# One ring of five 4 MB buffers for K, V and the weights of a decode step, in place of three pools of 1 and 2 MB buffers

## The chip, the cores and the metric

The kernel runs on one core of one Trainium2 chip. Times are microseconds (us) of device time, the median of several executions. "Before" is the kernel as it was, "changed" the kernel with the change. The span of a profile (first to last instruction) is up to about 2 us shorter than the reported time of the same execution.

## The reference, cut to what matters

One decode step for four sequences: attention over a cache of 8192 keys with 32 heads of 128, a gated feed-forward layer beside it, and a gate that mixes the two.

```python
# x: (4, 1, 1024)   k_cache, v_cache: (4, 32, 8192, 128) bf16, 268 MB each
q = (x @ wq).reshape(B, 1, 32, 128).transpose(0, 2, 1, 3)
p = softmax(einsum("bhqd,bhkd->bhqk", q, k_cache) * 128 ** -0.5)
a = einsum("bhqk,bhkd->bhqd", p, v_cache) ... @ wo            # wq, wo: 8.4 MB each
b = x + sigmoid(x @ w_r) * ((silu(x @ w_gate) * (x @ w_up)) @ w_down)   # 7.3 MB each
out = g * a + (1 - g) * b          # g = sigmoid(sum(x * gate_w))
```

Each K and V element is read once and used once. There are 575.7 MB to read and very little to compute on them.

## The kernel before

The parts that the change touches. Each of the 128 (sequence, head) units has one K transfer and one V transfer of 2 MB, in runs of 16 KB per partition. Weights come in 1 MB chunks, in runs of 1 KB (wq, gate, up) or 2 KB (down, wo).

```python
    GH = 8                                   # heads per softmax group
    LAG = GH + 3                             # V units behind K units
    wst = ctx.enter_context(tc.tile_pool(name="wst", bufs=3))
    knp = ctx.enter_context(tc.tile_pool(name="knp", bufs=2))
    vnp = ctx.enter_context(tc.tile_pool(name="vnp", bufs=3))
    # ... cut ...
        for b in range(Bn):                  # two-byte elements
            nc.sync.dma_start(out=xT[:, :, b], in_=x2[b].rearrange("(t c) -> c t", c=P))
        nc.sync.dma_start(out=wrg[:, :, 0], in_=B_w_r.rearrange("(t c) -> c t", c=P))
        nc.sync.dma_start(out=wrg[:, :, 1], in_=gate_w.rearrange("(t c) -> c t", c=P))
    # ... cut ...
    def w_in_chunk(view, c0, psum_view, t0):             # WCOLS = 512: 1 KB runs
        def emit():
            wc = wst.tile([P, DT, WCOLS], BF, tag="w")
            nc.sync.dma_start(out=wc[:], in_=view[:, :, c0:c0 + WCOLS])
            # ... 32 products of 128 x 128 weights with 4 columns ...
    # ... cut ...
    def k_unit(u):
        kn = knp.tile([P, J, Dh], BF, name="kn")
        nc.sync.dma_start(out=kn[:], in_=A_k_cache[b, h].rearrange("(p j) d -> p j d", p=P))
        T = ttp.tile([P, J, 2, 32, 2], BF, name="T")
        nc.vector.transpose(out=T[:]..., in_=kn[:]...)   # frees the K buffer
        # ... 16 products with T; at the 8th head of a group: softmax(g)
    def v_unit(u):
        vn = vnp.tile([P, J, Dh], BF, name="vn")
        nc.sync.dma_start(out=vn[:], in_=A_v_cache[b, h].rearrange("(p j) d -> p j d", p=P))
        # ... 16 products, a copy on ACT, 4 small products that transpose the head's output
```

The end of it: eleven V units without K units beside them, then wo in eight chunks, eight transposes, a copy and the output.

Of the kernel before, what the change touches and what calls it, by code (L numbers as in the profile page):

```python
# [9 lines left out]
BF = mybir.dt.bfloat16  # L10
F32 = mybir.dt.float32
# [8 lines left out]
def kernel(  # L20
# [14 lines left out]
):  # L35
    nc = tc.nc
# [4 lines left out]
    assert Sq == 1 and Dh == P and D % P == 0 and F % P == 0 and Sk % P == 0  # L41
    DT, FT, J = D // P, F // P, Sk // P
    GH = 8
    NJC = 4
    JJ = J // NJC
    assert J % NJC == 0 and JJ * 32 <= 512 and NJC * GH == 32 and JJ % 4 == 0
    LAG = GH + 3
    WPK = 2
    NU = Bn * H
    assert NU % GH == 0 and H % GH == 0 and H * Bn <= 128  # L50
    NG = NU // GH
    ZW = 128 * (GH - 1) + 31 + 128 + 1
# [5 lines left out]
    wst = ctx.enter_context(tc.tile_pool(name="wst", bufs=3))  # L58
    knp = ctx.enter_context(tc.tile_pool(name="knp", bufs=2))
    ttp = ctx.enter_context(tc.tile_pool(name="ttp", bufs=2))  # L60
    vnp = ctx.enter_context(tc.tile_pool(name="vnp", bufs=3))
    ptp = ctx.enter_context(tc.tile_pool(name="ptp", bufs=3))
    osp = ctx.enter_context(tc.tile_pool(name="osp", bufs=2))
    stat = ctx.enter_context(tc.tile_pool(name="stat", bufs=3))
    shrp = ctx.enter_context(tc.tile_pool(name="shrp", bufs=1, space=PSUM))
    scp = ctx.enter_context(tc.tile_pool(name="scp", bufs=2, space=PSUM))
    ops = ctx.enter_context(tc.tile_pool(name="ops", bufs=2, space=PSUM))
    o2p = ctx.enter_context(tc.tile_pool(name="o2p", bufs=2, space=PSUM))
    fps = ctx.enter_context(tc.tile_pool(name="fps", bufs=1, space=PSUM))

    ident = const.tile([P, P], BF)
    make_identity(nc, ident[:])
    identf = const.tile([P, P], F32)
    make_identity(nc, identf[:])
    R = const.tile([P, 4, P], BF)
    nc.gpsimd.memset(R[:], 0.0)
    for he in range(4):
        half, e = divmod(he, 2)
        nc.gpsimd.affine_select(out=R[:, he, :], in_=R[:, he, :], compare_op=ALU.not_equal, fill=1.0,
                                base=-(64 * half + e), pattern=[[0, 4], [-2, 32]], channel_multiplier=1)  # L80
    mask8 = const.tile([P, GH], F32)
    nc.gpsimd.memset(mask8[:], 0.0)
    for m in range(P // GH):
        nc.gpsimd.affine_select(out=mask8[:], in_=mask8[:], compare_op=ALU.not_equal, fill=1.0,
                                base=-GH * m, pattern=[[-1, GH]], channel_multiplier=1)
    pen8 = const.tile([P, GH], F32)
    nc.vector.tensor_scalar(out=pen8[:], in0=mask8[:], scalar1=-1.0, scalar2=3.0e38, op0=ALU.add, op1=ALU.mult)

    xT = const.tile([P, DT, Bn], BF)
    wrg = const.tile([P, DT, 2], BF)  # L90
    with nc.allow_non_contiguous_dma(reason="tiny transposed loads of x / w_r / gate_w"):
        for b in range(Bn):
            nc.sync.dma_start(out=xT[:, :, b], in_=x2[b].rearrange("(t c) -> c t", c=P))
        nc.sync.dma_start(out=wrg[:, :, 0], in_=B_w_r.rearrange("(t c) -> c t", c=P))
        nc.sync.dma_start(out=wrg[:, :, 1], in_=gate_w.rearrange("(t c) -> c t", c=P))
    wrep = const.tile([P, 2, DT, P], BF)
    for i in range(2):
        nc.vector.tensor_copy(out=wrep[:, i, :, :], in_=wrg[:, :, i:i + 1].to_broadcast([P, DT, P]))
# [4 lines left out]
    hT = const.tile([P, FT, Bn], BF)  # L103
    sgb = const.tile([P, 2, Bn], F32)
    c12 = const.tile([P, 2, Bn], F32)
    baseT = const.tile([P, DT, Bn], F32)
    Zt = [const.tile([P, 4, ZW], BF, name=f"Z{i}") for i in range(2)]
    for z in Zt:
        nc.gpsimd.memset(z[:], 0.0)

    shr = shrp.tile([P, 512], F32)
    nc.vector.memset(shr[:], 0.0)
    o0 = 0
    gu_ps = shr[:, o0:o0 + 2 * FT * Bn].rearrange("p (w t b) -> p w t b", w=2, t=FT); o0 += 2 * FT * Bn
    q_ps = shr[:, o0:o0 + H * Bn].rearrange("p (h b) -> p h b", h=H); o0 += H * Bn
    yT_ps = shr[:, o0:o0 + DT * Bn].rearrange("p (t b) -> p t b", t=DT); o0 += DT * Bn
    rg_ps = shr[:, o0:o0 + 2 * Bn].rearrange("p (w b) -> p w b", w=2); o0 += 2 * Bn
    aT_ps = shr[:, o0:o0 + DT * Bn].rearrange("p (t b) -> p t b", t=DT); o0 += DT * Bn
    assert o0 <= 512

    def mm_acc(out_ap, lhsT, rhs):
        nc.tensor.matmul(out_ap, lhsT=lhsT, rhs=rhs, start=False, stop=True, skip_group_check=True)  # L122

    for i in range(2):
        for t in range(DT):
            mm_acc(rg_ps[:, i, :], wrep[:, i, t, :], xT[:, t, :])
    nc.scalar.activation(out=sgb[:], in_=rg_ps, func=ACT.Sigmoid)
    nc.vector.tensor_scalar(out=c12[:, 0, :], in0=sgb[:, 1, :], scalar1=-1.0, scalar2=1.0, op0=ALU.mult, op1=ALU.add)
    nc.vector.tensor_tensor(out=c12[:, 1, :], in0=c12[:, 0, :], in1=sgb[:, 0, :], op=ALU.mult)

    WCOLS = 4 * P
    wqv = A_wq.rearrange("(t c) n -> c t n", c=P)
    wgv = B_w_gate.rearrange("(t c) f -> c t f", c=P)
    wuv = B_w_up.rearrange("(t c) f -> c t f", c=P)
    wdv = B_w_down.rearrange("(t f) n -> f t n", f=P)
    wov = A_wo.rearrange("(h d) n -> d h n", d=P)
    assert (H * Dh) % WCOLS == 0 and F % WCOLS == 0
    TCH = max(1, 4096 // D)

    def w_in_chunk(view, c0, psum_view, t0):  # L140
        def emit():
            wc = wst.tile([P, DT, WCOLS], BF, tag="w")
            nc.sync.dma_start(out=wc[:], in_=view[:, :, c0:c0 + WCOLS])
            for ci in range(WCOLS // P):
                for t in range(DT):
                    mm_acc(psum_view[:, t0 + ci, :], wc[:, t, ci * P:(ci + 1) * P], xT[:, t, :])
        return emit

    def w_out_chunk(view, r0, nrow, psum_view, rhs_of):
        def emit():  # L150
            wc = wst.tile([P, TCH, D], BF, tag="w")
            nc.sync.dma_start(out=wc[:, :nrow, :], in_=view[:, r0:r0 + nrow, :])
            for rr in range(nrow):
                for nt in range(DT):
                    mm_acc(psum_view[:, nt, :], wc[:, rr, nt * P:(nt + 1) * P], rhs_of(r0 + rr))
        return emit

    for h0 in range(0, H, WCOLS // P):
        w_in_chunk(wqv, h0 * P, q_ps, h0)()
    nc.vector.tensor_copy(out=qT[:], in_=q_ps)  # L160
    qa_ps = ops.tile([P, 4, H * Bn], F32, name="o_ps")
    for he in range(4):
        nc.tensor.matmul(qa_ps[:, he, :], lhsT=R[:, he, :], rhs=qT[:].rearrange("p h b -> p (h b)"),
                         start=True, stop=True)
    nc.vector.tensor_copy(out=qa[:].rearrange("p e h b -> p e (h b)"), in_=qa_ps[:])

    wjobs = []
    for f0 in range(0, FT, WCOLS // P):
        wjobs.append(("g", w_in_chunk(wgv, f0 * P, gu_ps[:, 0], f0)))
    for f0 in range(0, FT, WCOLS // P):  # L170
        wjobs.append(("u", w_in_chunk(wuv, f0 * P, gu_ps[:, 1], f0)))

    def h_job():
        g_sb = stat.tile([P, FT, Bn], F32, tag="g_sb")
        nc.scalar.activation(out=g_sb[:], in_=gu_ps[:, 0], func=ACT.Silu)
        nc.vector.tensor_tensor(out=hT[:], in0=g_sb[:], in1=gu_ps[:, 1], op=ALU.mult)
    wjobs.append(("h", h_job))
    for t0 in range(0, FT, TCH):
        wjobs.append(("d", w_out_chunk(wdv, t0, min(TCH, FT - t0), yT_ps, lambda t: hT[:, t, :])))

    def base_job():
        nc.vector.tensor_tensor(out=baseT[:], in0=xT[:], in1=c12[:, 0:1, :].to_broadcast([P, DT, Bn]), op=ALU.mult)
        ty = stat.tile([P, DT, Bn], F32, tag="ty")
        nc.vector.tensor_tensor(out=ty[:], in0=yT_ps, in1=c12[:, 1:2, :].to_broadcast([P, DT, Bn]), op=ALU.mult)
        nc.vector.tensor_tensor(out=baseT[:], in0=baseT[:], in1=ty[:], op=ALU.add)
    wjobs.append(("b", base_job))

    S_ps = {}
    PT_t = {}
    rinv_t = {}  # L190
    oT2_t = {}

    def build_strips(g):
        b, h0 = divmod(g * GH, H)
        Z = Zt[g % 2]
        for he in range(4):
            for a in range(4):
                c0 = 31 + 32 * a
                dst = Z[32 * a:32 * a + 32, he, c0:c0 + 128 * (GH - 1) + 1:128]
                nc.gpsimd.tensor_copy(out=dst, in_=qa[32 * a:32 * a + 32, he, h0:h0 + GH, b])  # L200

    def k_unit(u):
        b, h = divmod(u, H)
        g, h8 = divmod(u, GH)
        if h8 == 0:
            build_strips(g)
            S_ps[g] = scp.tile([P, JJ * 32], F32, name="S_ps")
        sps = S_ps[g]
        Z = Zt[g % 2]
        kn = knp.tile([P, J, Dh], BF, name="kn")  # L210
        nc.sync.dma_start(out=kn[:], in_=A_k_cache[b, h].rearrange("(p j) d -> p j d", p=P))
        T = ttp.tile([P, J, 2, 32, 2], BF, name="T")
        nc.vector.transpose(out=T[:].rearrange("p j h i e -> p (j h i e)").bitcast(U32),  # L213
                            in_=kn[:].rearrange("p j d -> p (j d)").bitcast(U32))
        n = 0
# [7 lines left out]
        if h8 == GH - 1:  # L223
            softmax(g)
# [129 lines left out]
```

## Time and profile before

| what | value | view |
|---|---|---|
| time | 1384.77 us (1384.01 to 1385.76) | times |
| DMA queue 1 | 575.71 MB, busy 99.5% of 16 engines | page, part 3 |
| PE, DVE | busy 82% and 44% of the span | page, part 1 |
| mean rate | 416 GB/s | page, part 2 |

This is the page's table of the span in 40 slices for the kernel before (busy tenths of the DMA engines, the rate in each slice, all packets by size), and the line of the queue that carries the data (packets, MB, share of 16 engines):

```profile
DMA  9999999999999999999999999999999999999997
GB/s 307 410 403 422 394 430 420 431 418 431 420 430 421 430 431 427 431 424 430 419 430 429 425 431 426 430 420 430 429 430 430 427 429 417 431 431 431 399 385 268
DMA packets 73973, 576.61 MB, mean 416 GB/s; under 512 B 10932, under 2 KB 33460, under 8 KB 41144
...
q1 hardware_dynamic: 73912, 575.71, 99.5%
```

The engines are "busy" all the time, so the busy share says nothing about what can be gained. The rate does: slices of 430 and 431 stand beside slices of 394 to 420. The view of stretches of the same kernel (stretch, length, busy time and count of PE, PE loads, DVE, ACT and POOL, granted clock, DMA share, GB/s) puts the losses into four places:

```profile
0.00:10.00 10.00, 0.75 (x16) 0.58 (x16) 2.47 (x6) 1.46 (x2) 1.20 (x9) 1.00 0.65 106
10.00:100.00 90.00, 52.99 (x765) 30.96 (x766) 27.83 (x9) 1.28 (x1) 18.28 (x56) 0.84 1.06 402
100.00:160.00 60.00, 43.57 (x372) 20.45 (x371) 30.89 (x19) 2.32 (x4) 4.18 (x18) 0.76 0.99 402
160.00:1300.00 1140.00, 983.02 (x4640) 443.17 (x4639) 549.44 (x261) 75.95 (x144) 55.00 (x237) 0.95 1.00 427
1300.00:1360.00 60.00, 52.09 (x272) 25.51 (x270) 1.41 (x6) 7.09 (x13) 0.40 (x1) 1.00 0.97 377
1360.00:1384.70 24.70, 9.74 (x273) 8.88 (x272) 1.24 (x4) 0.57 (x1) 0.00 (x0) 0.60 0.63 224
```

The loss in the middle is a small one at each of 16 softmaxes. In this piece of the timeline (start us, duration, engine, line, instruction, idle time before it and its releaser), DVE holds both K buffers while it waits for the group's maximum from POOL and the row sums from ACT; the next K transfer is issued only when the first late transpose ends:

```profile
670.91 0.69 DVE L229 TENSOR_REDUCE m_4110<-S_ps 128x1 f32<-128x512 f32 x1 [5.91 <-PE S_ps L220]
674.43 0.37 POOL L234 PARTITION_ALL_REDUCE gmx<-mex  x1
675.41 0.69 ACT L243 ACTIVATE PTs<-S_ps,negm 128x512 bf16<-128x512 f32 x1 [9.23 <-DVE negm L240]
677.10 8.72 DVE L213 STREAM_TRANSPOSE T<-kn 128x4096 uint32<-128x4096 uint32 x2
681.52 0.33 SPq L211 DMA_DIRECT2D kn<-in_A_k_cache_dram  x1
```

To compare kernels I use one more number, the **deficit**: a time on the trace less the time that the bytes moved so far would take at 431 GB/s (each packet's bytes spread over its recorded duration, the data queues alone). All 575.7 MB would take 1335.7 us, so the span of a kernel is 1335.7 us plus its final deficit. The kernel before has a deficit of 18.2 us at 160 us, 29.7 at 1300 us and 49.0 at its end.

### The profile page before, as it was taken

To read this page: it belongs to the slowest core of one execution; us is meant where nothing else is said; L and a number is where in the kernel's file an instruction comes from. 1 tells how busy PE (TensorE), PEld (TensorE's weight loads), DVE (VectorE), ACT (ScalarE), POOL (GpSimd) and SP (SyncE) were. 2 spreads that over 40 slices of the span, in tenths; PEclk is the share of its full clock that TensorE was granted. 3 is DMA by queue.
4 is the path that set the end of the run, shared out by engine and by line. 5 is a ranking of instruction groups with operands and counts; after the bars stand their busy time and mean duration, and the time that the engine had idled before them with its cause. 6 is when DMAs were issued, how large, how long until landed. Compare 5 with 4: busy or idle time off the path is not lost.

```text
span 1384.7 us, 14348 instructions
## 1 busy us (share of the span) xinstructions
PE 1142.2 (82%) x6332; PEld 529.5 (38%) x6332; DVE 613.3 (44%) x303; ACT 88.7 (6%) x165; POOL 79.1 (6%) x320
## 2 busy tenths in 40 slices
PE   2676889979797988979797997979797997989885
PEld 2333333434343433434343443434343343434443
DVE  1335545454535345444444445444454535354300
ACT  0000000000000000000000000000000000000110
POOL 3101010010101010010101000010101000000000
PEclk9877889999999999999999999999999999999997
DMA  9999999999999999999999999999999999999997
GB/s 307 410 403 422 394 430 420 431 418 431 420 430 421 430 431 427 431 424 430 419 430 429 425 431 426 430 420 430 429 430 430 427 429 417 431 431 431 399 385 268
DMA packets 73973, 576.61 MB, mean 416 GB/s; under 512 B 10932, under 2 KB 33460, under 8 KB 41144
## 3 DMA queue, kind: packets, MB, share of 16 engines
q1 hardware_dynamic: 73912, 575.71, 99.5%
q8 instruction: 49, 0.80, 0.2%
q14 instruction: 12, 0.10, 0.0%
HBM read 575.68 MB, written 0.01 MB: 416 GB/s over the span
## 4 chain that ended last, share of the span: by engine, by line
PE 61%; DMA 17%; DVE 10%; ACT 4%; POOL 4%; issue 3%; SPq 0%; ACTq 0%; DVEq 0%; POOLq 0%
PE S_ps L220 28%; PE o_ps L266 25%; DMA kn<-in_A_k_cache_dram 14%; DVE T L213 9%; ACT o_sb L270 4%; POOL Z_188 L200 2%; POOL Z_189 L200 2%; DMA wc<-in_A_wq_dram 1%; DMA wc<-in_A_wo_dram 1%; DVE PT L251 1%; PE oT_7480 L275 1%; PE shr L122 1%; PE oT_5562 L275 1%; PE oT_2338 L275 1%; PE oT_1935 L275 1%
## 5 line engine op out<-in xcount | busy, mean ns | idle before, releaser
L213 DVE STREAM_TRANSPOSE T<-kn 128x4096 uint32<-128x4096 uint32 x128 | 566.8, 4435 | 445.0 <-DMA kn<-in_A_k_cache_dram 434.8
L266 PE MATMUL o_ps<-vn,PT 128*4 128x512 bf16 x2048 | 463.2, 379 | 0.0
L220 PE MATMUL S_ps<-T,Z_188 128*128 128x512 bf16 x1024 | 264.5, 414 | 34.0 <-DVE T L213 34.0
L220 PE MATMUL S_ps<-T,Z_189 128*128 128x512 bf16 x1024 | 258.2, 407 | 35.2 <-DVE T L213 35.1
L266 PEld LDWEIGHTS <-PT 128*4 128x4 bf16 x2048 | 167.9, 87 | 280.5 <-issue 49.6
L220 PEld LDWEIGHTS <-Z_188 128*128 128x128 bf16 x1024 | 102.1, 104 | 167.5 <-issue 76.3
L220 PEld LDWEIGHTS <-Z_189 128*128 128x128 bf16 x1024 | 100.6, 102 | 164.3 <-issue 68.8
L270 ACT COPY o_sb<-o_ps 4x512 f32<-4x512 f32 x128 | 73.3, 572 | 1006.2 <-PE o_ps L266 1006.2
L200 POOL COPY Z_188<-qa 32x8 bf16<-32x8 bf16 x128 | 27.1, 211 | 529.5 <-PE S_ps L220 512.9
L200 POOL COPY Z_189<-qa 32x8 bf16<-32x8 bf16 x128 | 27.0, 211 | 499.0 <-PE S_ps L220 493.7
L122 PEld LDWEIGHTS <-wc 128*128 128x128 bf16 x1184 | 34.1, 101 | 54.5 <-DMA wc<-in_A_wq_dram 15.4
L122 PE MATMUL shr<-xT,wc 128*128 128x4 bf16 x704 | 21.8, 166 | 32.6 <-DMA wc<-in_A_wq_dram 14.7
L243 ACT ACTIVATE PTs<-S_ps,negm 128x512 bf16<-128x512 f32 x16 | 11.0, 687 | 165.1 <-DVE negm L240 165.1
L236 DVE TENSOR_TENSOR gmm<-gmx,mask_118 128x8 f32<-128x8 f32 x16 | 2.7, 167 | 41.7 <-POOL gmx L234 41.7
L282 DVE TENSOR_TENSOR OT<-oT_7480,rinv 128x8 bf16<-128x8 f32 x1 | 0.2, 176 | 42.5 <-PE oT_7480 L275 42.5
L122 PE MATMUL shr<-OT,wc 128*128 128x4 bf16 x256 | 7.8, 166 | 11.1 <-DMA wc<-in_A_wo_dram 11.1
L275 PE MATMUL oT_1532<-identf,o_sb 4*128 4x1 f32 x64 | 9.0, 258 | 7.2 <-ACT o_sb L270 7.2
L234 POOL PARTITION_ALL_REDUCE gmx<-mex x16 | 5.9, 368 | 156.4 <-DVE mex L232 148.8
L275 PE MATMUL oT_2338<-identf,o_sb 4*128 4x1 f32 x64 | 8.4, 248 | 7.3 <-ACT o_sb L270 7.3
L275 PE MATMUL oT_5562<-identf,o_sb 4*128 4x1 f32 x64 | 8.4, 248 | 7.3 <-ACT o_sb L270 7.3
L275 PE MATMUL oT_6368<-identf,o_sb 4*128 4x1 f32 x64 | 8.4, 248 | 7.3 <-ACT o_sb L270 7.3
L275 PE MATMUL oT_1935<-identf,o_sb 4*128 4x1 f32 x64 | 8.4, 248 | 7.3 <-ACT o_sb L270 7.3
(122 smaller groups left out, 302.5 us busy)
## 6 DMA issues: line engine op xcount, KB each, us to landing
kn<-in_A_k_cache_dram SPq DMA_DIRECT2D x128, 2048.0 KB, 14.8
vn<-in_A_v_cache_dram SPq DMA_DIRECT2D x128, 2048.0 KB, 16.3
wc<-in_A_wq_dram SPq DMA_DIRECT2D x8, 1024.0 KB, 7.7
wc<-in_A_wo_dram SPq DMA_DIRECT2D x8, 1024.0 KB, 8.5
wc<-in_B_w_gate_dram SPq DMA_DIRECT2D x7, 1024.0 KB, 11.9
wc<-in_B_w_up_dram SPq DMA_DIRECT2D x7, 1024.0 KB, 12.0
wc<-in_B_w_down_dram SPq DMA_DIRECT2D x7, 1024.0 KB, 11.6
xT<-in_A_x_dram SPq DMA_DIRECT2D x4, 2.0 KB, 3.2
```

Of the source, the lines that this page charges most:

```text
L122: nc.tensor.matmul(out_ap, lhsT=lhsT, rhs=rhs, start=False, stop=True, skip_group_check=True)
L200: nc.gpsimd.tensor_copy(out=dst, in_=qa[32 * a:32 * a + 32, he, h0:h0 + GH, b])
L213: nc.vector.transpose(out=T[:].rearrange("p j h i e -> p (j h i e)").bitcast(U32), in_=kn[:].rearrange("p j d -> p (j d)").bitcast(U32))
L220: nc.tensor.matmul(sps[:, :], lhsT=Z[:, he, s:s + P], rhs=T[:, JJ * jc:JJ * (jc + 1), half, :, e], start=(h8 == 0 and n == 0), stop=(h8 == ...
L234: nc.gpsimd.partition_all_reduce(gmx[:], mex[:], channels=P, reduce_op=bass_isa.ReduceOp.max)
L236: nc.vector.tensor_tensor(out=gmm[:], in0=gmx[:], in1=mask8[:], op=ALU.mult)
L243: nc.scalar.activation(out=PTs[:], in_=sps[:], func=ACT.Exp, bias=negm[:, 0:1], scale=scale, accum_out=rs[:, 0:1])
L251: nc.vector.transpose(out=PT[:].rearrange("p j c h -> p (j c h)"), in_=PTs[:])
L266: nc.tensor.matmul(o_ps[:, :], lhsT=PT[:, 4 * uq:4 * uq + 4, jc, h8], rhs=vn[:, j0:j0 + 4, :], start=(n == 0), stop=(n == J // 4 - 1))
L270: nc.scalar.copy(out=o_sb[:], in_=o_ps[:])
L275: nc.tensor.matmul(oT2[:, h8:h8 + 1], lhsT=o_sb[0:4, t * Dh:(t + 1) * Dh], rhs=identf[0:4, t:t + 1], start=(t == 0), stop=(t == 3))
L282: nc.vector.tensor_tensor(out=OT[:, h0:h0 + GH, b], in0=oT2[:, 0:GH], in1=rinv[:, :], op=ALU.mult)
```

## The change

Its intent: few, long transfers that never wait. K, V and all weights go through one pool of five 4 MB buffers. A piece of K or V is two heads, a contiguous 32 KB per partition; the weights are regrouped so that a partition reads 28 or 32 KB of contiguous rows (down 8 KB, wo still 2 KB). V follows K by four pieces. The small inputs become 16-byte runs and move to the ACT queue. The products that transpose a head's output are put off into the next piece, and wo and down multiply with the activations as the stationary side, so that the result needs no transposes at the end.

```diff
-    wst = ctx.enter_context(tc.tile_pool(name="wst", bufs=3))
-    knp = ctx.enter_context(tc.tile_pool(name="knp", bufs=2))
-    vnp = ctx.enter_context(tc.tile_pool(name="vnp", bufs=3))
+    ring = ctx.enter_context(tc.tile_pool(name="ring", bufs=5))
...
-            nc.sync.dma_start(out=xT[:, :, b], in_=x2[b].rearrange("(t c) -> c t", c=P))
-        nc.sync.dma_start(out=wrg[:, :, 0], in_=B_w_r.rearrange("(t c) -> c t", c=P))
+        nc.scalar.dma_start(out=xT[:], in_=x2.rearrange("b (c t) -> c b t", t=DT))
+        nc.scalar.dma_start(out=wrg[:, 0, :], in_=B_w_r.rearrange("(c t) -> c t", t=DT))
...
-            nc.sync.dma_start(out=wc[:], in_=view[:, :, c0:c0 + WCOLS])
+        w = slot()[:, :TW * H * Dh].rearrange("p (t h d) -> p t h d", t=TW, h=H)
+        nc.sync.dma_start(out=w.rearrange("p t h d -> p t (h d)"), in_=wqv[:, t0:t0 + TW, :])
...
+        return cache[b, h0:h0 + HT].rearrange("h (r j) d -> (h r) (j d)", j=JR)
...
-        kn = knp.tile([P, J, Dh], BF, name="kn")
-        nc.sync.dma_start(out=kn[:], in_=A_k_cache[b, h].rearrange("(p j) d -> p j d", p=P))
+        kn = slot()
+        nc.sync.dma_start(out=kn[:], in_=kv_view(A_k_cache, u))
+        for c in range(JR // CJ):            # four transposes per piece
...
-    while ik < NU: weights(WPK); k_unit(ik); ik += 1; v_unit(iv); iv += 1
+    for u in range(NT + LAG):
+        if u < NT:
+            k_piece(u)
+        if u >= LAG:
+            v_piece(u - LAG)
+        if side:
+            side.pop(0)()                    # one weight piece
+    for nh in (16, 12, 3, 1):                # wo, by heads
+        if h0 + nh <= H:
+            wo_piece(h0, nh)
...
```

(The removed loop is drawn together on one line; cuts are marked.)

## The prediction

> **What bounds the kernel now.** The DMA engines. In the queue view queue 1 is busy 99.5% of 16 engines (575.7 MB, mean 416 GB/s); PE is busy 82%, DVE 44%. The chain of waits names mostly PE (61%) because PE consumes last; in steady state the transfers end last (DVE waits 435 us for K). Where the mean loses to the best rate, 431 GB/s (225-265 and 620-665 us), by the view of stretches:
>
> - 0-10 us: 106 GB/s, 7.5 us lost. Six loads of x, w_r and gate_w in two-byte elements precede the first weights, issued only at 4.95 us.
> - 10-150 us: 383-409 GB/s, 11 us lost: weights in 1 KB runs (46 ns a packet against 611 ns for 16 KB, packet records: 38 ns per KB plus 8) and, at 140-145 us, 259 GB/s after the first softmax.
> - 150-1250 us: 427-428, about 9 us: at each of 16 softmaxes the two K buffers come free late (period 78.5 us for 33.55 MB, 77.9 at 431).
> - 1300-1360 us: 377 GB/s, 7.5 us: eleven V units left over, each 5.32 us on PE (3.6 of products, the ACT copy, transposing products), while their data needs 4.87 us.
> - 1360-1385 us: 224 GB/s, 12 us: wo waits for buffers, then transposes, output.
>
> Sum 47 us; 575.7 MB at 431 GB/s would be 1336 us.
>
> **What the change does.** Bytes stay. All streams share five 4 MB buffers, so a transfer waits for the piece five before it, which landed some 39 us (four pieces of 9.7 us) earlier. A K piece is freed after four transposes (8.9 us, 2 x 4.43 now), a V piece after 32 products (7.2 us at 226 ns): both far inside 39 us, so softmax should not reach the queue. Per pair of pieces (19.5 us) PE needs 14.4 us, DVE 8.9 plus softmax: neither becomes the limit. Weight runs grow to 8-32 KB (wo stays at 2). Small loads go to another queue. LAG falls to 4 pieces and the transposing products are put off, so a left-over V piece costs PE 7.2 us against 9.7 of DMA.
>
> **Sum.** Start 2.6 us (0.7 to issue, 1.9 to the first packet, as now). 575.7 MB at 431: 1335.7 us. The Trainium skill, "DMA: Bandwidth & Descriptors", section "Where 436 GB/s comes from", gives a ceiling of 435.2 GB/s; if what is missing at 16 KB is a fixed cost per packet, 32 KB gives 433, 1329.6 us. I take 432: 1332.6. wo's 2 KB runs: +0.6. Tail after the last landing: wo's 12-head piece lands 2.5 us before the end and needs 24 products, then 8 more: 32 x 0.226 = 7.2, so 4.7 us over; copy 0.7, output and end 2.6: 8 us. Total about 1343 us, 3% faster. All of it is on the critical path, since the DMA queue is that path.
>
> **What would show it.** Slices at 430-433 GB/s from first to last but one, no dip at softmax; K/V packets of 32 KB near 1210 ns; SyncE waiting for buffers with DMA full; weights at over 425 GB/s; only the last 8 us low.
>
> **What would make it wrong.** 32 KB runs that are slower or split (streams further apart in HBM), rate below 428; strided weight loads for gate/up, or a cold PE clock (0.5) making V pieces (32 x 0.43 = 13.7 us) and the wo tail slow; a dependence in the ring that serializes K and V; a queue that starves in the first pieces.
>
> Range 1333 to 1356 us. Chances: faster by over 2% 0.86, within 2% 0.12, slower 0.02.

## The result

The changed kernel takes 1361.18 us (1361.15 to 1361.58, four runs), the kernel before 1384.94 us in the same rounds; the ratio is 0.9835, with a 95% interval of 0.9821 to 0.9849. It is 1.6 to 1.7% faster. The prediction was 1343 us with a range of 1333 to 1356, so it was 18 us too low.

The page of the changed kernel, the same lines:

```profile
DMA  9999999999999999999999999999999999999996
GB/s 398 389 431 430 428 430 431 432 430 430 431 431 430 430 430 431 432 431 431 430 431 431 431 431 431 431 431 431 431 432 431 431 430 430 430 430 431 430 425 237
DMA packets 25278, 576.49 MB, mean 424 GB/s; under 512 B 3068, under 2 KB 3076, under 8 KB 7176
...
q1 hardware_dynamic: 24392, 575.68, 98.9%
```

The middle is flat now, as predicted: no dips at the softmaxes. The busy share fell a little while the kernel became faster. What is left is at the two ends. The stretches of the changed kernel:

```profile
0.00:10.00 10.00, 0.00 (x0) 0.00 (x0) 0.48 (x1) 1.28 (x1) 0.86 (x6) 1.00 0.91 351
10.00:40.00 30.00, 0.00 (x0) 0.00 (x0) 0.00 (x0) 0.00 (x0) 4.68 (x12) 1.00 0.99 421
40.00:60.00 20.00, 12.35 (x281) 8.46 (x282) 6.22 (x13) 1.46 (x2) 1.56 (x8) 1.00 0.91 358
60.00:160.00 100.00, 82.32 (x718) 41.89 (x717) 53.91 (x32) 3.94 (x6) 6.53 (x27) 0.88 1.01 430
160.00:1300.00 1140.00, 970.52 (x4228) 408.85 (x4226) 559.55 (x351) 60.79 (x103) 70.55 (x269) 0.94 1.00 431
1300.00:1330.00 30.00, 25.26 (x128) 12.11 (x129) 0.24 (x1) 2.30 (x4) 0.00 (x0) 1.00 0.99 416
1330.00:1359.90 29.90, 25.46 (x104) 9.79 (x103) 0.92 (x2) 1.15 (x2) 0.00 (x0) 0.89 0.60 217
```

The line of 10 to 40 us shows the first surprise: PE and DVE did nothing at all in it, though the first weights (4 MB) had landed by 14 us, by the semaphore times. The deficits, stage by stage, of the two kernels (and of the two best experiments, told below):

| stage | before | changed | x_first | tail8 |
|---|---|---|---|---|
| 0 to 160 us | 18.2 | 7.2 | 4.3 | 4.3 |
| 160 to 1300 us | 11.5 | 1.6 | 1.5 | 1.5 |
| 1300 us to the end | 19.3 | 15.4 | 14.5 | 12.1 |
| span less 1335.7 us | 49.0 | 24.2 | 20.3 | 17.9 |

So the change won 11.0 us at the start, 9.9 in the middle and 3.9 at the end.

### The profile page after: what moved, and what is told of

Same layout as the page of the kernel before. It is cut to its first block, busy times and chain, and to the rows that moved or that the text cites. A ratio compares the mean times of both kernels' runs of the same rounds, so it can differ in the third digit from the quotient of the medians. Undisturbed runs are those within 1.5% of the kernel's fastest.

```text
span 1359.9 us, 12458 instructions
## 1 busy us (share of the span) xinstructions
PE 1115.9 (82%) x5456; PEld 481.1 (35%) x5456; DVE 621.3 (46%) x399; ACT 70.9 (5%) x118; POOL 84.2 (6%) x322
## 4 chain that ended last, share of the span: by engine, by line
DMA 44%; PE 39%; DVE 11%; issue 4%; ACT 1%; POOL 0%; ACTq 0%; DVEq 0%
DMA piece<-in_A_k_cache_dram 38%; PE S_ps L252 17%; PE o_ps L304 17%; DVE T L245 11%; DMA wrg<-in_B_w_r_dram 3%; DMA piece<-in_A_wo_dram 3%; PE acc L140 2%; PE shr L140 2%; PE oT L317 1%; ACT o_sb L310 1%; DVE OT L322 0%; DVE wrep L146 0%; POOL PB_128 L282 0%; ACT PTs L275 0%; DVE PT L277 0%
## 5 line engine op out<-in xcount | busy, mean ns | idle before, releaser
L245 DVE STREAM_TRANSPOSE T<-piece 128x2048 uint32<-128x2048 uint32 x256 | 577.3, 2291 | 487.9 <-DMA piece<-in_A_k_cache_dram 390.0
L252 PE MATMUL S_ps<-T,Z_126 128*128 128x512 bf16 x1024 | 281.8, 429 | 92.9 <-DVE T L245 92.6
L252 PE MATMUL S_ps<-T,Z_127 128*128 128x512 bf16 x1024 | 264.0, 408 | 54.5 <-DVE T L245 54.5
L304 PE MATMUL o_ps<-piece,PB_129 128*8 128x512 bf16 x1024 | 227.9, 381 | 2.0 <-DMA piece<-in_A_v_cache_dram 1.9
L304 PE MATMUL o_ps<-piece,PB_128 128*8 128x512 bf16 x1024 | 226.2, 379 | 0.0
L304 PEld LDWEIGHTS <-PB_129 128*8 128x8 bf16 x1024 | 86.9, 87 | 139.0 <-issue 16.3
L304 PEld LDWEIGHTS <-PB_128 128*8 128x8 bf16 x1024 | 86.4, 87 | 137.3 <-issue 13.6
L317 PE MATMUL oT<-ident,o_sb 8*128 8x2 f32 x512 | 67.1, 249 | 46.3 <-ACT o_sb L310 46.3
L317 PEld LDWEIGHTS oT<-ident,o_sb 8*128 8x128 f32 x512 | 61.6, 186 | 78.5 <-ACT o_sb L310 78.5
L310 ACT COPY o_sb<-o_ps 8x512 f32<-8x512 f32 x64 | 36.7, 574 | 923.0 <-PE o_ps L304 923.0
L236 POOL COPY Z_126<-qa 32x4 bf16<-32x4 bf16 x128 | 24.9, 195 | 567.8 <-PE S_ps L252 523.0
L236 POOL COPY Z_127<-qa 32x4 bf16<-32x4 bf16 x128 | 24.9, 194 | 549.6 <-PE S_ps L252 544.1
L140 PEld LDWEIGHTS <-piece 128*128 128x128 bf16 x704 | 22.5, 112 | 2.9 <-issue 2.0
L140 PE MATMUL shr<-xT,piece 128*128 128x4 bf16 x704 | 22.6, 171 | 0.2 <-issue 0.2
L277 DVE STREAM_TRANSPOSE PT<-PTs 128x512 bf16<-128x512 bf16 x16 | 11.4, 712 | 13.5 <-ACT PTs L275 13.5
```

Of the source, the lines that this page charges most:

```text
L140: nc.tensor.matmul(out_ap, lhsT=lhsT, rhs=rhs, start=start, stop=True, skip_group_check=True)
L236: nc.gpsimd.tensor_copy(out=Z[32 * a:32 * a + 32, :, 31 + 32 * a:32 + 32 * a], in_=qa[32 * a:32 * a + 32, :, h0 + a // QH, b:b + 1])
L245: nc.vector.transpose(out=T[:].rearrange("p j h i e -> p (j h i e)").bitcast(U32), in_=kn[:, c * CJ * Dh:(c + 1) * CJ * Dh].bitcast(U32))
L252: nc.tensor.matmul(sps[:, :], lhsT=Z[:, he, s:s + P], rhs=T[:, 16 * jl:16 * jl + 16, half, :, e], start=(t == 0 and jc == 0 and he == 0), ...
L277: nc.vector.transpose(out=PT[:].rearrange("p j i -> p (j i)"), in_=PTs[:])
L304: nc.tensor.matmul(o_ps[:, :], lhsT=B_[:, JC * t + jc, uq].rearrange("p s j -> p (s j)"), rhs=vn[:, j0 * Dh:(j0 + 4) * Dh], start=(n == 0) ...
```

## The experiments

I made seventeen runs, all correct by the check against the reference (which is not sharp for this input: two runs below mix the keys of two heads). Differences among the variants of the changed kernel are read from their own medians, which agree within 2.2 us among the four executions of each (within 0.5 for the changed kernel, x_first and tail8), and from their traces. The runs were made on four chips (chip 7 for eight of them, 5 for four, 3 for three, 10 for flat16 and flat8); the plateau with 32 KB packets was 430.4 GB/s on chips 3, 5 and 7 alike. The times of the kernel before ranged from 1379.9 to 1390.5 us in these rounds, so I don't compare variants by their ratios to it.

### What held the start up: x behind 32 KB packets

These lines are of the changed kernel: first ACT's queue, with packets, MB and share, then from its timeline the issue of x, the ninth DMA issue of the kernel (the fifth on the SyncE queue) and PE's first instruction, then what the SyncE queue waited for (us in total, times, longest):

```profile
q10 hardware_dynamic: 832, 0.02, 0.0%
```

```profile
0.79 0.46 ACTq L90 DMA_DIRECT2D xT<-in_A_x_dram  x1
0.80 0.85 SPq L169 DMA_DIRECT2D piece<-in_A_wq_dram  x2
40.05 0.33 SPq L242 DMA_DIRECT2D piece<-in_A_k_cache_dram  x1
43.14 0.38 PE L140 MATMUL shr<-xT,wrep 128*128 128x4 bf16 x8 [43.14 <-DVE wrep L146]
```

```profile
SPq L242 <- DMA xT<-in_A_x_dram: 37.3, 1, 37.3
```

x was issued at 0.79 us and landed at 40 us. It consists of 16-byte packets; with w_r and gate_w there are 768, 48 for each of the 16 engines. In the packet records 520 of them, 32.5 an engine, are spread evenly over the 36 us from 3.6 to 39.5 us, one per engine every 1.1 us, among packets of 1.2 us on the other queue. The other 248 went through in about 2 us, up to 41.8 us, when the other queue had run empty. The Trainium skill, page "DMA: Bandwidth & Descriptors", section "Queues, rings and completion order", says that an engine goes round its queues packet by packet. That fits: each packet of the small queue waits for a turn, and a turn is about as long as the other queue's packet. The consequences were two: the ninth transfer reuses the completion semaphore of x, so its issue waited 37 us for it; and PE could not start, so the buffers filled and stayed full. Two experiments test this from both sides.

**x_first.** One load moves to the head of the SyncE queue.

```diff
-        nc.scalar.dma_start(out=xT[:], in_=x2.rearrange("b (c t) -> c b t", t=DT))
+        nc.sync.dma_start(out=xT[:], in_=x2.rearrange("b (c t) -> c b t", t=DT))
```

> The changed kernel with one small load, x in 16-byte runs, put on the SyncE queue ahead of the first weights instead of on the ACT queue. Theory: on the ACT queue its 512 short packets get one turn per 32 KB packet of the other queue, so x lands only at 40 us; the ninth DMA issue waits for it (37 us) and PE starts at 43 us, so the queue runs empty twice between 40 and 60 us, 3.4 us in all. With x first it should land before 6 us, the first weights start 0.5 us later, and the deficit at 60 us against 431 GB/s falls from 6.4 to about 3.5 us: 1358 us. Rival (the queue is held up there by the ring and PE's weight work and not by x): 1361 us, the dip at 40 to 60 us stays.

Measured: 1357.86 us, 3.3 less than the changed kernel. x's packets ran from 1.9 to about 2.3 us, the deficit at 60 us fell from 6.4 to 3.5 us, and the hole is gone from the stretches of this run:

```profile
40.00:60.00 20.00, 14.57 (x150) 7.82 (x148) 10.30 (x5) 0.00 (x0) 0.79 (x4) 0.76 1.00 428
```

**wq8.** x stays where it is; only the first two pieces of the other queue get shorter packets (four rows of 8 KB with a 64-byte gap in the buffer).

```diff
-        return ring.tile([P, RING], BF, name="piece", tag="piece")
+        return ring.tile([P, RING + 128], BF, name="piece", tag="piece")
...
-        w = slot()[:, :TW * H * Dh].rearrange("p (t h d) -> p t h d", t=TW, h=H)
+        w = slot()[:].rearrange("p (t x) -> p t x", t=TW)[:, :, :H * Dh].rearrange("p t (h d) -> p t h d", h=H)
```

> The changed kernel with only the two wq pieces, the first 8 MB of all, in 8 KB runs instead of 32 KB; the small loads stay on the ACT queue. This tells the cause of their lateness. Theory (one short packet of the ACT queue gets a turn for each packet of the other queue): 48 short packets per engine at one per 0.31 us put x on the chip at about 17 to 20 us instead of 40, PE starts before 25 us, the two holes at 40 to 60 us vanish, and the time is 1358 us. Rival (16-byte transfers are slow in themselves, or the ACT queue is): x still lands near 40 us and the time stays at 1361 us.

Measured: 1359.12 us. The 768 short packets were through at 20.1 us instead of 41.8, without being touched; PE started at 18.9 us; the deficit at 60 us was 3.8 us. So it is the length of the other queue's packets that made x late, not the 16-byte transfer and not the ACT queue.

### What the ring's depth is worth

**ring4, ring3, ring3_x.** `bufs=5` becomes 4 or 3; the third also has x first.

> The changed kernel with a ring of four buffers. Theory: a buffer comes free within about 20 us of its landing, four pieces are 39 us, so four are enough for the plateau at 430 to 431 GB/s; the 16 engines can drift apart less (8.3 us between first and last engine's landing of one piece with five), which should cost nothing or gain a little at the end; the first hole comes earlier (four pieces are landed at 39 us, PE starts at 43), so about 2 us more there if x is as late: 1361 to 1364 us. Rival (depth of five is what holds the plateau): plateau below 428, over 1370 us.

> The changed kernel with a ring of three buffers. If depth is what the change is worth, three pieces, of which one is being consumed by DVE or PE at any time, leave one or two in flight: at the softmaxes, where DVE stands for about 5 us and V waits for the probabilities, the queue should run empty as in the kernel before, the plateau fall to about 420 to 427 GB/s and the time rise to 1375 to 1395 us with 32 KB runs kept. If the runs are what the change is worth, it stays within 6 us of 1361.

> Three buffers instead of five, with x loaded first. Three buffers alone cost 13.5 us, of which the trace puts 13.2 us between 30 and 50 us, when all buffers are full and PE still waits for x, and 3 us after the first softmax, while the plateau stayed at 430 GB/s. Theory: depth was needed only to live through the late x, so with x first three buffers take 1358 plus about 3 to 5 us, 1361 to 1363. Rival (depth matters in itself): still over 1370 us.

Measured: ring4 1370.97 us, ring3 1374.72 us, ring3_x 1360.58 us. Both theories of the first two runs were wrong in the same way. The times rose by 9.8 and 13.5 us, but not because the plateau fell. The stretches of ring4:

```profile
40.00:50.00 10.00, 6.05 (x87) 2.72 (x88) 2.60 (x9) 0.18 (x1) 0.00 (x0) 1.00 0.04 10
50.00:60.00 10.00, 6.62 (x202) 5.83 (x200) 4.10 (x4) 1.28 (x1) 1.56 (x8) 1.00 0.80 308
200.00:1250.00 1050.00, 890.23 (x3858) 374.65 (x3857) 516.71 (x327) 56.16 (x95) 67.31 (x258) 0.93 1.00 431
```

With four buffers all of them are full at 39 us, and nothing is transferred until PE has x and has consumed the first weights: 10 GB/s for 10 us. I had expected 2 us there; the deficit grew by 13.0 us from 40 to 60 us, against 3.4 with five buffers. The plateau is 431 with four and 430 with three. With x first, three buffers lose only 2.7 us against five. So depth was mostly an insurance against the late x, and for the softmaxes three buffers of 4 MB are nearly enough.

**before_k3.** The kernel before with a third K buffer, nothing else: `name="knp", bufs=2` becomes `bufs=3`.

> The kernel before with three K buffers instead of two, 16 KB runs and all else unchanged. Theory 2 (buffers): the loss of about 0.7 us at each softmax comes from K buffers that come free late; between 160 and 1300 us the kernel before lost 11.5 us against 431 GB/s and this one should lose under 3, so 1376 us. Theory 1 (run length): the loss there comes from 16 KB packets, and a third buffer leaves 1385 us.

Measured: 1379.59 us (1377.94 to 1382.25), against 1383.77 for the kernel before in these rounds; ratio 0.9962, interval 0.9931 to 0.9993. The same stretch, before and then before_k3:

```profile
160.00:1280.00 1120.00, 964.46 (x4550) 434.85 (x4548) 539.26 (x254) 74.81 (x142) 54.63 (x236) 0.95 1.00 427
160.00:1280.00 1120.00, 963.48 (x4567) 434.54 (x4567) 541.00 (x255) 74.81 (x142) 54.64 (x236) 0.96 1.01 430
```

The deficit from 160 to 1280 us grew by 4.7 us, against 11.4 for the kernel before. From 100 to 160 us, where the first softmax lies, it grew by 1.2 instead of 4.2 us. So most of the loss in the middle was the K buffers, as theory 2 said, though not all of the 8.5 us that were expected; 2.8 us were given back after 1280 us (4.6 us were lost between 1280 and 1300 us). (These are single traces of a kernel whose time varies by several us; the medians differ by 4.2 us.) Packets stayed at 16 KB, and between 160 and 600 us this kernel held 429.9 GB/s.

### What the length of a run is worth

The prediction took 431 GB/s as what 16 KB runs reach and hoped for 433 with 32 KB. **runs8, runs2, runs16** keep the ring, the order and the arithmetic, and lay each K and V piece down as 4, 16 or 2 blocks per partition with 64-byte gaps, so that a transfer of 4 MB is made of shorter packets. The core of the edit (NBLK blocks of BLK elements):

```diff
-        return ring.tile([P, RING], BF, name="piece", tag="piece")
+        return ring.tile([P, RING + 32 * NBLK], BF, name="piece", tag="piece")
...
+    def blocks(tile_):
+        return tile_[:].rearrange("p (n x) -> p n x", n=NBLK)[:, :, :BLK]
...
-        nc.sync.dma_start(out=kn[:], in_=kv_view(A_k_cache, u))
+        nc.sync.dma_start(out=blocks(kn), in_=kv_view(A_k_cache, u).rearrange("p (n x) -> p n x", n=NBLK))
```

> The changed kernel with every K and V piece laid into its buffer as four blocks of 8 KB per partition with a 64-byte gap, so that the same single 4 MB transfer is made of 8 KB runs instead of 32 KB; buffers, order and arithmetic as they are. Theory 1 (the long runs pay, because each packet has a fixed cost): the packet records say 309 ns for 8 KB against 1213 ns for 32 KB, that is 424 against 432 GB/s; 537 MB of K and V would take about 23 us more, 1384 us, and the gain over the kernel before would be gone. Theory 2 (the deep ring pays, and the fixed cost of a packet is hidden behind the packets next to it): 1361 us, within 3 us, the plateau still at 430 to 431 GB/s.

> As the run with 8 KB, but sixteen blocks of 2 KB per partition. Theory 1 (fixed cost per packet): 84 ns for 2 KB is 390 GB/s by the records, so about 130 us more, near 1490 us. Theory 2 (cost mostly hidden): the 1 KB weights of the kernel before still ran at 408 GB/s, so 2 KB should lie between 408 and 431, about 420: some 33 us more, near 1394 us. If 2 KB runs leave the time at 1361, run length does not matter at all from 2 KB up.

> The changed kernel with every K and V piece laid down as two blocks of 16 KB per partition: the run length of the kernel before in the buffers of the changed one. The run with 8 KB came out at 424 GB/s and 1378 us, that with 2 KB at 398 and 1463, just what their packet records of 309 and 82 ns say. Theory A (a fixed cost of 7 to 9 ns a packet up to some size, and another limit near 431 GB/s above it): 16 KB already stands at 430 to 431, as the kernel before did between softmaxes, so 1361 us within 2 us, and 16 to 32 KB buys nothing. Theory B (the cost per packet goes on halving): 16 KB lies halfway between 424 and 431, 428 GB/s, about 1367 us.

Measured: 1377.93, 1463.23 and 1371.23 us. Theory 2 fell (8 KB was not within 3 us of 1361; its plateau is the 424 GB/s of theory 1; an earlier x, with a deficit at 60 us of 3.7 instead of 6.4 us, and a plateau to start from of 430.4 instead of 432 kept the time under 1384; with 2 KB the plateau of 397 lay between the two expectations), and so did theory A: the plateau with 16 KB is the 428 of theory B. (4 of the 10 us of this run are a larger hole at 50 to 60 us, where x was late again.) Length counts at every size. But the kernel before and before_k3 had 16 KB packets at 430 GB/s between softmaxes, so I suspected the 64-byte gaps. **runs16a, runs8a** widen the gaps to 256 bytes (`RING + 128 * NBLK`); **flat16, flat8** have no gaps, and get short runs by taking the source from two or four places:

```diff
-        return cache[b, h0:h0 + HT].rearrange("h (r j) d -> (h r) (j d)", j=JR)
+        return cache[b, h0:h0 + HT].rearrange("h s d -> (h s d)").rearrange("(q p x) -> p q x", q=2, p=P)
...
-        nc.sync.dma_start(out=kn[:], in_=kv_view(A_k_cache, u))
+        nc.sync.dma_start(out=kn[:].rearrange("p (q x) -> p q x", q=2), in_=kv_view(A_k_cache, u))
```

> As the run with 16 KB blocks, but with gaps of 256 bytes between the blocks instead of 64. If the number of packets is the cause (6.9 ns a packet plus 37.8 ns per KB fits 2, 8 and 16 KB), the plateau between 200 and 1250 us stays at 428.4 GB/s and the time at 1371 us. If the odd block addresses are the cause, the plateau rises to 430 GB/s and the time falls by about 6 us.

> As the run with 8 KB blocks, but with gaps of 256 bytes. Number of packets: plateau 423.8 GB/s and 1378 us as before. Addresses: plateau over 428 GB/s and about 1364 us or less (x lands early enough with 8 KB packets, so 1358 to 1360 is possible).

> x first, and every K and V piece moved in 16 KB runs without gaps: a partition gets 16 KB of one head and 16 KB of the other. The result is wrong on purpose (keys of two heads are mixed); instructions, sizes and order are the same. Reference is x first with 32 KB runs, 1357.9 us and a plateau of 430.4 GB/s between 200 and 1250 us. If the number of packets is the cost (6.9 ns each), the plateau is 428.4 and the time 1364 us. If the gaps were, the plateau is 430 and the time 1358 to 1359 us.

> The same with 8 KB runs, four places a partition, no gaps, wrong result on purpose. Number of packets: plateau 423.8 GB/s, about 1377 us. Gaps: plateau over 429 GB/s, under 1362 us. In between, the split says how much each is.

Measured: runs16a 1374.64, runs8a 1387.16, flat16 1367.20, flat8 1386.83 us. (The flat runs have x first; their reference is 1357.86.) The same stretch of two traces, x_first and then flat8:

```profile
200.00:1250.00 1050.00, 892.54 (x3874) 376.01 (x3873) 519.61 (x324) 55.88 (x94) 66.06 (x253) 0.94 1.00 431
```

```profile
200.00:1250.00 1050.00, 883.30 (x3788) 370.77 (x3787) 506.31 (x322) 56.17 (x95) 66.88 (x254) 0.93 1.01 421
```

All of them, from the packet records between 200 and 1250 us (rate with each packet's bytes spread over its duration; "per packet" is size x 16 engines / rate):

| run | packet | gap | GB/s | ns per packet |
|---|---|---|---|---|
| changed, x_first | 32 KB | none | 430.4 | 1218.1 |
| flat16 | 16 KB | none | 427.2 | 613.7 |
| runs16a | 16 KB | 256 B | 427.2 | 613.7 |
| runs16 | 16 KB | 64 B | 428.4 | 611.9 |
| before_k3 (160 to 600 us) | 16 KB | one run per partition | 429.9 | 609.7 |
| flat8 | 8 KB | none | 420.8 | 311.5 |
| runs8a | 8 KB | 256 B | 420.7 | 311.5 |
| runs8 | 8 KB | 64 B | 423.8 | 309.3 |
| runs2 | 2 KB | 64 B | 397.1 | 82.5 |

The layouts without gaps and with 256-byte gaps agree to 0.1 ns, and 8, 16 and 32 KB lie on one line: 311.5, 613.7 and 1218.1 ns are 9.3 ns plus 37.78 ns per KB (302.2 for 8 KB more, then 604.4 for 16 KB more). So in these layouts there is a fixed cost per packet, 9.3 ns. Gaps of 64 bytes made it smaller, 6.9 ns (2, 8 and 16 KB fit 6.9 plus 37.8 per KB), the opposite of what I suspected; why is open. Also open is why the layout of the kernel before, one 16 KB run per partition in each transfer, is about 4 ns a packet cheaper than flat16. If it is set beside the 32 KB packets, which are also one run per partition, the two give only about 1.3 ns a packet plus 38.0 ns per KB; so the line above is not a rule for every layout. What it means for the change: in the ring's layout, halving the run costs 9.3 us (flat16 less x_first), but against the kernel before, whose 16 KB packets went at 609.7 ns in before_k3, doubling the run saved 0.1% of K and V.

**w1k.** x first, and wq, gate and up in 1 KB runs as the kernel before had them (blocks of 512 elements with 32-byte gaps); K and V stay at 32 KB.

```diff
-        nc.sync.dma_start(out=w.rearrange("p t h d -> p t (h d)"), in_=wqv[:, t0:t0 + TW, :])
+        nc.sync.dma_start(out=w, in_=wqv[:, t0:t0 + TW, :].rearrange("c t (m x) -> c (t m) x", x=512))
```

> x first, and the weights wq, gate and up (23 MB) in 1 KB runs as the kernel before had them, all else as changed. The kernel before lost 6.4 us against 431 GB/s between 10 and 100 us. Theory: the part of that that comes from run length is 23 MB at 408 instead of 431 GB/s, 2.9 us: 1361 us, and the rest came from its three small weight buffers and its two K buffers. Rival (all of it is run length): 1364 us or more. If 1358, run length of the weights was worth nothing.

Measured: 1369.08 us, 11.2 more than x_first, and the deficit at 160 us was 14.8 instead of 4.3 us. I had expected 2.9: the 408 GB/s that I took for 1 KB runs was read from a stretch that mixes them with 16 KB K transfers. By the cost per packet, 23.1 MB in 1 KB packets are 22,528 packets, 1,408 for each engine, and 10.5 us spread over them are 7.5 ns each, in line with the table.

But this is not what the 1 KB runs cost the kernel before. Where each of the two kernels moves nothing but 1 KB packets (two stretches of before, then one of w1k), the kernel before is faster:

```profile
10.00:20.00 10.00, 4.06 (x128) 3.73 (x128) 0.00 (x0) 0.00 (x0) 9.66 (x15) 1.00 1.09 387
20.00:30.00 10.00, 3.04 (x96) 2.79 (x96) 0.17 (x1) 0.00 (x0) 1.86 (x10) 1.00 1.08 383
10.00:20.00 10.00, 7.15 (x132) 3.83 (x132) 2.00 (x4) 0.00 (x0) 4.68 (x12) 1.00 1.10 357
```

At 385 GB/s a 1 KB packet takes 42.6 ns, 4.5 ns more than at 431, and 1,408 of these are 6.4 us. All 1 KB packets of the kernel before lie before 100 us, and from 10 to 100 us its deficit grew by just these 6.4 us. So in the kernel before the short weight runs were worth at most about 6 us, not the 11.2 of w1k, whose 1 KB packets (other addresses on both sides, with 32-byte gaps in the buffer) are slower for a reason that stays open. The 11.0 us that the change won before 160 us come in three parts: 4.8 us in the first 10 us, where the weights start earlier; 2.6 us from 10 to 100 us (6.4 against 3.8, of which the late x took 3.4); and 3.6 us from 100 to 160 us, where before_k3 puts 3.0 on the K buffers.

### What bounds the end

In the changed kernel the last V piece landed at 1330.1 us. Its timeline from there:

```profile
1330.09 8.75 PE L304 MATMUL o_ps<-piece,PB_129 128*8 128x512 bf16 x32 [1.91 <-DMA piece<-in_A_v_cache_dram]
1338.94 0.57 ACT L310 COPY o_sb<-o_ps 8x512 f32<-8x512 f32 x1 [11.85 <-PE o_ps L304]
1340.85 15.66 PE L140 MATMUL acc<-piece,OT 128*4 128x512 bf16 x64 [0.24 <-DMA piece<-in_A_wo_dram]
1356.33 0.68 DVE L350 CAST res<-acc 4x512 bf16<-4x512 f32 x1 [15.44 <-PE acc L140]
```

That is a chain of 29.8 us (1359.9 less 1330.1) on PE. The last loads landed at 1351 us and did not matter. Some 3 us of the chain are PE's clock: the 32 products of V took 8.75 us, though those of the piece before took 7.07, and the 64 with wo took 15.66, though tail8 below does them in 14.3. In both groups the first products start 0.43 us apart and the later ones 0.22. These are stretches of the changed kernel, then one of tail8 (the third number from the end is the granted clock):

```profile
1330.00:1335.00 5.00, 4.91 (x15) 1.65 (x15) 0.00 (x0) 0.00 (x0) 0.00 (x0) 0.66 0.95 336
1340.00:1345.00 5.00, 4.76 (x18) 1.98 (x18) 0.24 (x1) 0.00 (x0) 0.00 (x0) 0.66 1.03 360
1330.00:1340.00 10.00, 8.98 (x46) 3.93 (x44) 0.24 (x1) 0.57 (x1) 0.00 (x0) 1.00 1.02 361
```

Two things made the last V piece late. One is everything above. The other is that the 16 DMA engines drift apart. A transfer counts as landed when the last engine is done, and the times of its 16 semaphore increments show how far apart they are: 1.3 us at the start of the changed kernel, 5.2 in the middle, 8.3 near 1300 us and 9.3 for the last V piece. In the kernel before, with shorter queues, it stays at 2 to 3 us; in ring3 and ring3_x, with three buffers, it was 4.5 to 4.7 us near 1300 us. When the last V piece landed, the first engines had already moved 2.0 MB of wo (its 2 KB packets are seen from 1320 us on), 4.5 us worth at 431 GB/s.

This looks like engines of unequal speed, but the trace says otherwise. The page of the changed kernel has a queue of another kind:

```profile
q8 instruction: 42, 0.69, 0.2%
```

These are 42 packets of 16 KB, each about 1 us long and, by the queue's name, of the program's own instructions. From one landing to the next, between 130 and 1305 us, the engines' distances from the first one either stand still (68 of 105 steps) or grow by about 1.6 us in sum (37 steps). Each of the 33 instruction packets in that time falls into a step that grows, and 36 of the 37 have one. Near 1300 us nine engines are 5.7 to 8.3 us behind the first, and the other six within 2.5. No run without these packets was made, so the cause is read from the times and not tested.

**wo_early.** wo of heads 0 to 19 ahead of the last two V pieces, the last V piece in two transfers.

```diff
+            if u - LAG == NT - 3:
+                wo_piece(0, 16)
+            if u - LAG == NT - 2:
+                wo_piece(16, 4)
...
-    h0 = 0
-    for nh in (16, 12, 3, 1):
+    h0 = 20
+    for nh in (8, 3, 1):
```

> The changed kernel with the output weights of heads 0 to 19 loaded and multiplied before the last two V pieces, the last V piece in two transfers, and heads 20 to 31 after it. Theory: after the last V piece landed (1330 us) the end is a chain on PE: 8.8 us of products, 1.7 us of copy and transposing products, 64 products with wo in 15.7 us, 3.3 us of output; the transfers end 9 us before the kernel does. With 24 instead of 64 products left and half of V done, the chain after the last V piece is 3.6 + 1.7 + 5.4 + 3.3 = 14 us, that piece lands about 8 us before the transfers end, and the kernel ends about 6 us after them: 1358 us. Rival (the tail is bound by transfers, by wo in 2 KB runs and by engines that finish at different times): 1361 us, PE waiting for wo.

Measured: 1363.0 us, 1.8 more. The chain moved rather than shrank: the last but one V piece now landed at 1334.4 us and was multiplied whole until 1342.8, so the last one, landed by 1344.2, was through only at 1350.8, and the 24 products left ended at 1357.8. Neither theory described it.

**tail_fine and tail8.** x first, the order left alone, the last V piece in two transfers, wo in finer pieces.

```diff
-        nc.sync.dma_start(out=vn[:], in_=kv_view(A_v_cache, u))
+        nj = RING // 2 if u == NT - 1 else RING
+        for j in range(0, RING, nj):
+            nc.sync.dma_start(out=vn[:, j:j + nj], in_=kv_view(A_v_cache, u)[:, j:j + nj])
...
-    for nh in (16, 12, 3, 1):
+    for nh in (8, 8, 8, 4, 3, 1):            # tail8; tail_fine has (16, 6, 6, 3, 1)
```

> A version meant to beat both: x first, the last V piece in two transfers, wo in pieces of 16, 6, 6, 3 and 1 heads instead of 16, 12, 3 and 1; order of pieces unchanged. With x first alone the last V piece landed at 1327.3 us, PE was done with it and its outputs at 1338.0, with wo of 16 heads at 1345.0, waited until 1345.9 for the 12-head piece and was done at 1353.0, while the transfers ended at 1348.5. Theory: half of the last V piece is multiplied before its second half lands (4 to 5 us earlier through with V), and six-head pieces are used as they land, so PE ends about 1350.5 instead of 1353 and the kernel takes about 1355.5 us. Rival (the tail is bound by the slowest DMA engine alone): within 0.5 us of 1357.9.

> As tail_fine, with wo in pieces of 8, 8, 8, 4, 3 and 1 heads. In tail_fine the outputs were ready at 1336.1 us, but PE waited until 1338.3 for the 16-head piece and then needed 15.5 us for 64 products without a pause. Theory (the chain outputs, 64 products, output): with an 8-head piece landed by about 1335, PE goes on at 1336 and ends by 1351, kernel at about 1356 us against 1359.1. Rival (the tail is bound by the slowest DMA engine's share of wo): PE stops between wo pieces and the time stays at 1358 or above.

Measured: tail_fine 1359.07 us, tail8 1355.27 us. In tail_fine the outputs were ready at 1336.1 us, earlier than in x_first (1337.7), but the 16-head piece of wo had not landed on the last engine until 1338.3, and 64 products in one row followed (15.52 us, the first ones again 0.43 us apart). tail8 takes wo as it lands:

```profile
1333.32 1.05 PE L319 MATMUL oT<-ident,o_sb 8*128 8x2 f32 x8 [0.72 <-ACT o_sb L312]
1334.29 3.61 PE L140 MATMUL acc<-piece,OT 128*4 128x512 bf16 x16
1338.21 3.61 PE L140 MATMUL acc<-piece,OT 128*4 128x512 bf16 x16 [0.30 <-DMA piece<-in_A_wo_dram]
1343.52 7.07 PE L140 MATMUL acc<-piece,OT 128*4 128x512 bf16 x32 [1.70 <-DMA piece<-in_A_wo_dram]
```

PE now stops for wo at 1338.2 and 1343.5 us, so the end is near the DMA's own: the last load landed at 1348.7 us, PE was done at 1350.6, the kernel at 1353.6. tail8 beats both kernels: 0.9785 of the kernel before in its rounds (0.9759 to 0.981), and 5.9 us less than the changed kernel by their medians. Not all of this is the finer pieces: tail8's granted clock was 1.00 from 1305 us on, while in x_first it was 0.71 from 1325 to 1330 us and the 32 products of the last V piece took 8.60 us instead of 7.07. So of the 2.6 us between x_first and tail8 up to 1.5 can be the clock; no run separates the two.

## Why the prediction was wrong

It had the right bound and most of the mechanism. DMA is the limit; the dips at the softmaxes vanished (the deficit from 160 to 1300 us fell from 11.5 to 1.6 us); PE and DVE did not become the limit in the plateau; 32 KB packets take 1215 ns in the median and 1218 in the mean, predicted near 1210. The 18 us come from terms of its sum, and three steps failed: the rate that longer runs would give, the small loads taken as free, and the tail:

| term | predicted | measured | missed |
|---|---|---|---|
| 575.7 MB on the plateau | 1332.6 us at 432 GB/s | 1335.7 plus 2.4 lost from 60 to 1300 us, a plateau of 430.4 | 5.5 |
| start | 2.6 | 3.0 | 0.4 |
| x late, two holes at 40 to 60 us | 0 | 3.4 (x_first won back 3.3) | 3.4 |
| wo's transfers and the tail | 0.6 + 8 | 6.4 + 9.0 | 6.8 |
| reported time less span | 0 | 1.3 | 1.3 |
| sum | 1343.8 | 1361.2 | 17.4 |

- **"at 431 ... if what is missing at 16 KB is a fixed cost per packet, 32 KB gives 433".** The base was too high and the condition did not hold for the kernel before. I read 431 for 16 KB from stretches of 40 and 45 us in a view that rounds (430.5 in both), counts a packet's bytes where it starts, and counts the instruction packets as well (0.4 and 0.9 GB/s here). The data alone, with the bytes spread over each packet, moved at 430.0 and 428.9 in these stretches. In before_k3 16 KB packets went at 609.7 ns, and 32 KB packets at 1218.1 ns in the changed kernel: twice the length saved 0.1%, and the plateau was 430.4 and not 432. (In the ring's other layouts the fixed cost is real, and their line extrapolates to 16 x 1024 / 37.78 = 433.7 GB/s, near the ceiling of 435.2 that the Trainium skill states in "DMA: Bandwidth & Descriptors", section "Where 436 GB/s comes from"; no run here has packets over 32 KB, so none shows where the limit lies.)
- **"Small loads go to another queue", taken as free.** It was an error in the mechanism and not in a size: I listed "a queue that starves in the first pieces" among the dangers and gave it no time. wq8 shows that a short packet waits for a turn of the other queue's packet, and x_first that this cost 3.3 us.
- **"Tail after the last landing".** The prediction let PE keep up with wo as it landed, so that only 32 products were left after the 12-head piece. In fact PE began the 64 products with wo 10.8 us after the last V piece had landed and never caught up with the transfers. Of the 6.8 us, 4.5 are the late landing of that V piece, which comes with the last engine while the others already move wo. The other 2.3 are the chain on PE from there, 29.8 us instead of the 27.5 that follow from the prediction's figures (19.5 for wo at 431 GB/s and 8 after it); the reduced clock, which the prediction had named among the dangers, is worth more than that.
- **Not in the sum, but wrong:** the share of weights in 1 KB runs in the loss. I put 11 us on these runs and the first softmax together, and took 408 GB/s for 1 KB later on; the kernel before lost about 6 us to the runs (w1k, with other addresses, 11.2).

Of the 24.8 us that the span fell, before_k3 assigns about 10 to K buffers that come free in time (3.0 before 160 us and 6.7 after). About 6 are the weights' longer runs, by the rate and the deficit in the trace of the kernel before; w1k shows that run length costs time in the ring, but not this size. The late x took 3.4 back. The rest, 4.8 us in the first 10 us, some 4 in the middle and 3.9 at the end, I only read from the traces and did not test part by part.

## What to carry to other kernels

When the DMA engines are busy all the time, look at the rate and not at the busy share, and count packets: the runs that are worth lengthening may be a small part of the bytes (here 4% of them gave about a quarter of the gain). A tiny load that everything depends on belongs at the head of the queue that carries the long packets, not on a second queue beside it. Deep prefetch lets the DMA engines drift apart, so look at how far apart one transfer's semaphore increments lie before you plan the end; small last pieces, used as they land, gave the best time here.

## What the Trainium skill lacked or had wrong

- Page "DMA: Bandwidth & Descriptors", sections "Queues, rings and completion order" and "Rules for kernel authors": it says that queues interleave packet by packet and that a second issuing engine doesn't help bandwidth. It lacks the consequence that a load of short packets waits for one long packet per turn: 48 short packets per engine took until 41.8 us beside 32 KB packets and until 20.1 us when the first 8 MB beside them were in 8 KB packets.
- The same page, "Specifications", has 512 bytes as the least transfer for line rate, and "Why small descriptors are slow (HBM only)" treats packets of 256 bytes. Here 2 KB packets ran at 397.1 GB/s, 8 KB at 420.8 to 423.8 and 32 KB at 430.4, so the rate still rose by 8% from 2 KB on: 6.9 to 9.3 ns a packet in the ring's layouts.
- No page that I read gives a time for the layout's effect on that cost: gaps of 64 bytes between blocks took 309.3 ns for 8 KB, gaps of 256 bytes and no gaps 311.5 ns.
- No page that I read says what instruction packets do to a stream of data: in the changed kernel 33 of 16 KB each fell into steps in which the engines moved about 1.6 us apart, and the landing of one piece spread from 1.3 to 8.3 us over 1300 us.
